# Attention and feed-forward on one core: transposes of q, k and x of batches 4 to 8 moved from TensorE to the DMA, and a reordered start

## The chip, the cores and the metric

The kernel runs on one core of a Trainium2 chip. The metric is the device time of one execution in microseconds (us). The profile's span is a little shorter than that time (348.7 us where the profiled program took about 350), because it counts from the first to the last recorded event. Engines are named as in the profile: PE is TensorE (PEld its weight loads), DVE is VectorE, ACT is ScalarE, POOL is GpSimd, SP is the engine that here only issues DMAs. A "q" behind a name (SPq) is that engine's instruction queue. The text counts batches from 1, the code from 0.

## The reference, cut to what matters

```python
# q, k, v: (8, 8, 576, 64), moe_w_in: (512, 2048), moe_w_out: (2048, 512), float32
scores = scale * np.matmul(q, k.transpose(0, 1, 3, 2))
# heads 0..3 ("plain"):   key is one of the last 32 positions
# heads 4..7 ("dilated"): key is one of the last 128 positions, and (q - k) % 4 == 0
scores = np.where(masks[None, :, :, :], scores, -1e9)
attn = softmax(scores)                       # cut
x = np.matmul(attn, v).transpose(0, 2, 1, 3).reshape(4608, 512)
h = x @ w_in
return (h * sigmoid(h)) @ w_out              # (4608, 512) float32
```

Two things follow. Scores need q and k with the 64 head elements on the partitions, and `x @ w_in` needs x with its 512 features on the partitions; what comes from memory and what attention gives has tokens on the partitions. So q, k and x have to be transposed. And only a narrow band of scores is needed, so attention is small beside the feed-forward part: 1152 matmuls of 512 columns.

## The kernel before: the parts that matter here

All steps of attention (transposes, scores, products with v) and all steps of the feed-forward part (four matmuls each) are put into one order for TensorE by a small plan inside the kernel. The plan simulates engines with given step lengths and given arrival times of the loads. TensorE then runs its instructions strictly in that order, so a step that the plan placed too early holds up everything behind it.

```python
ARRIVE = {0: (8.5, 15.0), 1: (33.0, 47.0)}      # the plan's arrival of q,k and of v, batches 1 and 2
AT_WIN = [19.5, 22.0, 24.5, 27.0]
AT_WOUT = [36.0, 38.5, 41.0, 43.5]
...
def trans_d(ring, h):                            # q and k of a dilated head: 6 transposes on TensorE
    tps = small(ring, [P, 2, 3, MA], F16, f"td_{b}_{h}")
    for rp in range(2):
        for i, key in enumerate(("k", "rest", "q")):
            nc.tensor.transpose(tps[:, rp, i], loads[b][key][:, HN + h, 2 * rp : 2 * rp + 2, :],
                                ident[:MA, :MA])
    yield "DVE", 0.40
    nc.vector.tensor_copy(kqD[:, h]..., tps...)  # PSUM to SBUF
# trans_a, trans_b: 24 transposes a batch for the plain heads, copied on ACT
# x_p, x_d: 28 transposes a batch of the attention output x, copied on DVE (first batch: ACT)
...
def scores(ring, u):                             # matmuls, exp on ACT, then the mask:
    nc.vector.tensor_tensor(pm, pm, mk, ALU.mult)
...
def l1(f):                                       # feed-forward, first layer: a group of 512 tokens
    for c in range(HP):
        nc.tensor.matmul(h, w_in16[:, c, f * P : (f + 1) * P], xT[:, c, t0 : t0 + GT], ...)
    # tanh on ACT, product on DVE into gT
```

So TensorE does 48 transposes of q and k and 28 of x in every batch. All loads are issued by POOL, as DMAs that also cast float32 to float16.

The softmax here doesn't subtract the row's maximum and nothing guards it: scores larger than these inputs give would overflow.

## Time and profile before

| | before |
|---|---|
| time, median of 3 runs | 349.93 us |
| span of the profile | 348.7 us |
| TensorE busy | 325.1 us (93%) |
| first feed-forward matmul | 29.3 us |
| feed-forward matmuls between 100 and 200 us | 349 of 1152 |

The first lines of the profile's page: busy time of each engine, then rows of 40 slices of the span, each digit a tenth of the slice; PEclk is the clock granted to TensorE. The last line is from the chain that ended last.

```profile
PE 325.1 (93%) x2656; PEld 165.1 (47%) x2656; DVE 221.7 (64%) x602; ACT 168.5 (48%) x322; POOL 53.1 (15%) x74
PE   0688898999989999999999999999999999999995
PEclk9999998999999999999999999999999999999999
DMA  8999999929913972990589110100111200201232
PE 84%; DVE 9%; ACT 3%; DMA 2%; issue 1%; POOL 1%; ACTq 0%; POOLq 0%
```

TensorE is the limit: from about 105 us on its row shows nothing but nines until the last slice. The DMA engines are nearly full in the first 70 us and mostly idle from about 190 us on. That idle resource is what the change wants to use.

The timeline of TensorE at the start (start us, length us, line, operation, out<-in, shapes, count, and in brackets the idle time before it with what ended it), and one piece of the chain near the end. `h` and `y` are the two feed-forward layers, `td`, `ta`, `tb` transposes of q and k, `xp`, `xd` of x, `s` the scores, `av` the products with v:

```profile
11.30 0.24 PE L290 MATMUL td_0_205<-ident,rest_111 96*128 96x96 f16 x1 [4.41 <-DMA rest_111<-in_q_dram]
...
29.28 1.90 PE L498 MATMUL h_0_520<-xT,w_in_83 128*128 128x512 f16 x4
30.97 1.91 PE L498 MATMUL h_1_525<-xT,w_in_83 128*128 128x512 f16 x4
...
341.18 3.47 PE y_3_4542 L526 x16
```

TensorE waits until 11.3 us for the last of q and k, and starts its first feed-forward step at 29.3 us. The starts of the first two steps lie 1.69 us apart, against 0.86 us for the same four matmuls later (3.45 us for 16): until then TensorE ran at half speed. The Trainium skill, "TensorE: Matmul & The Clock Gate", section "What's actually happening", says that half clock is the default state and that sustained activity over a window of about 3.4 us releases it. This trace agrees with the two levels, 1.69 and 0.86 us.

### The profile page before, as it was taken

To read this page: it belongs to the slowest core of one execution; us is meant where nothing else is said; L and a number is where in the kernel's file an instruction comes from. 1 tells how busy PE (TensorE), PEld (TensorE's weight loads), DVE (VectorE), ACT (ScalarE), POOL (GpSimd) and SP (SyncE) were. 2 spreads that over 40 slices of the span, in tenths; PEclk is the share of its full clock that TensorE was granted. 3 is DMA by queue.
4 is the path that set the end of the run, shared out by engine and by line. 5 is a ranking of instruction groups with operands and counts; after the bars stand their busy time and mean duration, and the time that the engine had idled before them with its cause. 6 is when DMAs were issued, how large, how long until landed. Compare 5 with 4: busy or idle time off the path is not lost.

```text
span 348.7 us, 6693 instructions
## 1 busy us (share of the span) xinstructions
PE 325.1 (93%) x2656; PEld 165.1 (47%) x2656; DVE 221.7 (64%) x602; ACT 168.5 (48%) x322; POOL 53.1 (15%) x74
## 2 busy tenths in 40 slices
PE   0688898999989999999999999999999999999995
PEld 0553444555445455445554555455545444444442
DVE  4394777758888895888498739883986255054100
ACT  1453664076457546554644464546554254244211
POOL 8724344020203302030311000000000000000000
PEclk9999998999999999999999999999999999999999
DMA  8999999929913972990589110100111200201232
GB/s 107 188 205 199 200 181 169 189 53 141 109 30 37 178 55 59 132 120 32 89 127 103 31 36 27 32 32 30 32 31 32 60 11 22 77 14 32 61 82 70
DMA packets 59920, 29.80 MB, mean 85 GB/s; under 512 B 26608, under 2 KB 55280, under 8 KB 59888
## 3 DMA queue, kind: packets, MB, share of 16 engines
q0 software_dynamic: 54256, 19.92, 51.5%
q1 hardware_dynamic: 5632, 9.44, 9.1%
q8 instruction: 21, 0.34, 0.4%
q14 instruction: 11, 0.09, 0.1%
HBM read 39.84 MB, written 9.44 MB: 141 GB/s over the span
## 4 chain that ended last, share of the span: by engine, by line
PE 84%; DVE 9%; ACT 3%; DMA 2%; issue 1%; POOL 1%; ACTq 0%; POOLq 0%
DMA rest_111<-in_q_dram 2%; DVE gT_1066 L509 1%; PE y_1_892 L526 1%; PE y_3_3599 L526 1%; PE y_3_3089 L526 1%; PE y_3_2568 L526 1%; PE y_2_965 L526 1%; PE y_0_2117 L526 1%; PE y_0_664 L526 1%; PE y_3_4542 L526 1%; PE y_2_2464 L526 1%; PE y_2_2984 L526 1%; PE y_1_3338 L526 1%; PE y_1_3848 L526 1%; PE y_2_3495 L526 1%; PE y_3_1985 L526 1%
## 5 line engine op out<-in xcount | busy, mean ns | idle before, releaser
L498 PEld LDWEIGHTS <-w_in_83 128*128 128x128 f16 x576 | 52.8, 98 | 57.2 <-issue 6.1
L526 PEld LDWEIGHTS <-gT_4055 128*128 128x128 f16 x64 | 6.3, 98 | 7.5
L526 PEld LDWEIGHTS <-gT_3654 128*128 128x128 f16 x64 | 6.3, 98 | 7.6
L526 PEld LDWEIGHTS <-gT_4267 128*128 128x128 f16 x64 | 6.2, 97 | 7.6
L526 PEld LDWEIGHTS <-gT_3144 128*128 128x128 f16 x64 | 5.9, 98 | 6.4
L526 PEld LDWEIGHTS <-gT_519 128*128 128x128 f16 x64 | 5.8, 101 | 6.3 <-issue 1.4
L105 POOL DMA_DIRECT2D vraw_100<-in_v_dram x8 | 5.4, 678 | 20.7 <-DVE vd_98 L359 18.3
L105 POOL DMA_DIRECT2D vraw_101<-in_v_dram x8 | 5.4, 678 | 20.5 <-DVE vd_99 L359 14.7
L526 PEld LDWEIGHTS <-gT_1066 128*128 128x128 f16 x64 | 5.7, 98 | 5.8 <-DVE gT_1066 L509 0.4
L526 PEld LDWEIGHTS <-gT_2629 128*128 128x128 f16 x64 | 5.6, 97 | 5.1
L526 PEld LDWEIGHTS <-gT_2070 128*128 128x128 f16 x64 | 5.6, 97 | 5.1
L526 PEld LDWEIGHTS <-gT_1525 128*128 128x128 f16 x64 | 5.5, 97 | 4.9
L290 PE MATMUL td_0_205<-ident,k_nat_115 96*128 96x96 f16 x2 | 0.5, 272 | 6.6 <-DMA k_nat_115<-in_k_dram 6.6
L121 POOL DMA_DIRECT2D vp_97<-in_v_dram x4 | 5.7, 1432 | 1.5 <-DMA q_nat_167<-in_q_dram 1.4
L121 POOL DMA_DIRECT2D vp_96<-in_v_dram x4 | 5.8, 1444 | 0.6 <-PE td_3_678 L290 0.5
L290 PEld LDWEIGHTS <-rest_111 96*128 96x128 f16 x32 | 3.5, 108 | 5.1 <-issue 4.5
L311 PEld LDWEIGHTS <-kP_106 64*128 64x128 f16 x96 | 3.1, 100 | 5.7 <-issue 5.4
L273 ACT COPY kP_106<-ta_0_224 128x384 f16<-128x384 f16 x1 | 0.5, 479 | 10.9 <-PE ta_0_224 L270 10.9
L509 DVE SCALAR_TENSOR_TENSOR gT_4267<-th_0_4281,h_0_4268 128x512 f16<-128x512 f32 x1 | 0.7, 689 | 7.9 <-ACT th_0_4281 L507 7.9
L328 PEld LDWEIGHTS <-kqD_105 64*128 64x128 f16 x128 | 2.9, 97 | 5.8 <-issue 5.1
L365 PEld LDWEIGHTS <-probs_86 128*128 128x128 f16 x48 | 4.1, 100 | 3.1 <-DVE o_d_199 L368 0.8
L328 PEld LDWEIGHTS <-kqD_104 64*128 64x128 f16 x128 | 3.2, 102 | 5.2 <-issue 4.7
(1782 smaller groups left out, 1014.7 us busy)
## 6 DMA issues: line engine op xcount, KB each, us to landing
w_in_83<-in_moe_w_in_dram POOLq DMA_DIRECT2D x4, 512.0 KB, 12.1
w_out_84<-in_moe_w_out_dram POOLq DMA_DIRECT2D x4, 512.0 KB, 16.2
vp_97<-in_v_dram POOLq DMA_DIRECT2D x4, 384.0 KB, 10.8
vp_96<-in_v_dram POOLq DMA_DIRECT2D x3, 384.0 KB, 6.4
vraw_100<-in_v_dram POOLq DMA_DIRECT2D x4, 224.0 KB, 5.5
vraw_101<-in_v_dram POOLq DMA_DIRECT2D x4, 224.0 KB, 8.3
rest_111<-in_k_dram POOLq DMA_DIRECT2D x4, 192.0 KB, 6.2
rest_111<-in_q_dram POOLq DMA_DIRECT2D x4, 192.0 KB, 7.7
```

The costliest lines, as they stand in the source:

```text
L105: nc.gpsimd.dma_start(out=vraw[p0 : p0 + m1 - m0, ab].rearrange("p h r d -> p h (r d)"), in_=src[m0:m1],)
L121: nc.gpsimd.dma_start(out=vp[:, j0:, :D], in_=win)
L273: nc.scalar.copy(kt[:, :MA], tps[:, 0].rearrange("p r m -> p m r"))
L290: nc.tensor.transpose(tps[:, rp, i], loads[b][key][:, HN + h, 2 * rp : 2 * rp + 2, :], ident[:MA, :MA],)
L311: nc.tensor.matmul(sp[i][:, QB * jj : QB * (jj + 1)], kP[r, hp, QB * j : QB * j + P], qP[r, hp, :, QM * j : QM * (j + 1)], start=True, sto ...
L328: nc.tensor.matmul(sp[i][:, c : c + MH], kqD[r, h, rp, 0, ab * KB : ab * KB + P], kqD[r, h, rp, 1, ab * MH : (ab + 1) * MH], start=True, s ...
L365: nc.tensor.matmul(a[:, i, : D + 1], lhs(i), rhs(i), start=True, stop=True)
L498: nc.tensor.matmul(h, w_in16[:, c, f * P : (f + 1) * P], xT[:, c, t0 : t0 + GT], start=(c == 0), stop=(c == HP - 1),)
L509: nc.vector.scalar_tensor_tensor(gTs[g][:, f], th, 1.0, h, ALU.add, ALU.mult)
L526: nc.tensor.matmul(y, gTs[g][:, f, tb * P : (tb + 1) * P], w_out16[:, f], start=(f == 0), stop=(f == NFF - 1),)
```

## The change

Its intent: take the transposes of the last five batches off TensorE and give them to the DMA, which has time; and start the feed-forward part sooner. The parts:

- q and k of batches 4 to 8 are cast by a DMA into scratch memory in DRAM (`kq_s`) and come back through four transposing DMAs a batch. The plain heads are read as overlapping rows of 128 elements, so that two heads can use the two halves of TensorE's rows.
- x of batches 4 to 8 is stored to DRAM scratch (`x_s`) and comes back transposed, one DMA a feed-forward group.
- The first batch comes in two halves (dilated heads first), its mask is added into the scores by a matmul with the identity before `exp` instead of a multiply on DVE after it, and the first 512 tokens of the feed-forward part are two groups of 256.
- Loads are reordered, and the stores of the output go from SP to ACT.
- In all batches: scores are put into other sets, a copy out of PSUM goes to DVE or ACT as the plan has time, x is kept in the order of tokens, and attention may run further ahead of the feed-forward part.

The core of the diff:

```diff
+    GROUPS = [(0, GT // 2), (GT // 2, GT // 2)] + [(t, GT) for t in range(GT, NT, GT)]
+    PEB = 3                     # q, k: batches 0..2 on TensorE
+    PEX = 3                     # x: the same
+    BIASED = (0,)
...
+    def issue_cast(b):
+        for i, src in enumerate((k, q)):
+            nc.gpsimd.dma_start(out=kq_s[b][i]..., in_=src[b]...)
+    def issue_turn(b, n):       # n = 0..3: plain k, plain q, dilated k, dilated q
...
+            nc.sync.dma_start_transpose(out=dst[:, None, :], in_=win)
...
+            nc.sync.dma_start_transpose(out=kqTs[b % 2][:, i], in_=rows)
...
-    issue_qk(0)
+    issue_first(HN, H)
     make_identity(nc, ident)
...
+    issue_first(0, HN)
...
+    AT_DIL = {0: 7.6, 1: 33.5, 2: 53.0}
+    AT_PLAIN = {0: 11.0, 1: 33.5, 2: 53.0}
+    AT_WOUT = [38.0, 40.5, 47.5, 50.0]
...
+    def turn_gen(b):
+        for n, us in enumerate((3.0, 3.0, 1.5, 7.5)):
+            issue_turn(b, n)
+            yield "DMA", us
...
+    def loads_gen(b):
+        last = max(b - 1, PEB)
+        for i in range(2):      # POOL waits here until the batch before is transposed
+            nc.gpsimd.tensor_copy(fence[:, i : i + 1], kqTs[last % 2][:, i, 1, HN * M - 1 :])
+        if b - 2 >= PEX:
+            nc.gpsimd.tensor_copy(fence[:, 2:3], x_of(first_of[b - 2])[:, HP - 1, GT - 1 :])
+        issue_vraw(b)
+        issue_vp(b)
+        if b > PEB:
+            issue_cast(b)
...
+            if biased:
+                for i in range(2):
+                    nc.tensor.matmul(sp[i]..., ident, bs, start=True, stop=False)
...
-                nc.sync.dma_start(out=rows[r, m : m + n], in_=ob[p : p + n])
+            nc.scalar.dma_start(out=out[t0 + tb * P : t0 + (tb + 1) * P], in_=ob)
```

## The prediction

> **What bounds the kernel now.** TensorE. The engine table gives it 325.1 of 348.7 us; the chain of waits puts 84% of the span on it, 9% on VectorE, 2% on DMA. The granted clock is near 1.0 throughout. 1152 matmuls of 512 columns are needed whatever the change does; the 16 of one y tile take 3.45 us in the undisturbed end of the kernel, 0.216 us each, together 248.5 us. The other 100 us are, by start-to-start differences in the timeline:
> - attention on TensorE, 7 to 7.3 us a batch where nothing waits (stretch 208 to 243): 1.85 for the products with v, 1.89 for the scores, and 3.35 for transposes (q, k: 0.69 + 0.44 + 1.11; x: 0.58 + 0.53). Eight batches: 58 us;
> - the start: the first feed-forward matmul begins at 29.3 us, with only about 7 us of warm-rate work done, so 22 us are lost. The q, k loads end at 11.2 us and delay everything;
> - slow first feed-forward matmuls (four-matmul steps of 1.71 us instead of 0.86), waits up to 100 us and small waits later: about 15 us;
> - the end, last matmul to last byte: 4 us.
>
> **What the change does.**
> 1. Batches 4 to 8 lose all 76 transposes a batch on TensorE, and their PSUM copies on VectorE and ScalarE: 5 x 3.35 = 16.7 us of TensorE time, on the critical path because TensorE never idles after 100 us.
> 2. The DMA takes them over: per batch 1.77 MB of q, k (the plain heads written twice) and 0.59 MB of x through transposing DMAs, plus a cast through DRAM. The Trainium skill, "DMA: Bandwidth & Descriptors", section "Latency and other measured facts", gives 261 GB/s for a transposing DMA in one kernel; estimate 9 us a batch, perhaps 15 with latencies, against a cadence of 35.6 us per group. The slices show DMA 10% to 20% busy from 200 us on and about 60% busy in 100 to 180, so it should fit. The trace of before has no transposing DMA, so this step is the least certain.
> 3. First batch: half of q, k comes first, so transposes start near 7 us instead of 11.3; the first group has 256 tokens and needs half a batch. I expect the first feed-forward matmul at 20 us, bounded by v and the first quarter of w_in. 9 us earlier, but 4 us of attention move behind it and the bias matmuls cost 1 to 2 us. Net 3 to 4 us, and 3 to 5 us fewer waits up to 100 us, since loads are ordered by need.
> 4. VectorE and ScalarE lose work (masks of batch 1, pairing, transposed copies): not critical, worth 1 us. New waits on transposing DMAs, and ScalarE issuing the output stores: minus 1 to 3 us.
>
> **Sum.** 350 - 16.7 - 3.5 - 4 - 1 + 2 = about 326; with some further gain from the longer lead of attention, 324 us. Range 314 to 335. Faster by over 2%: 0.93; within 2%: 0.05; slower: 0.02.
>
> **What would show it.** TensorE instructions down by 380 in transposes (2656 to about 2330, the narrower first groups and bias matmuls adding some); steady groups of 512 tokens at about 32 us instead of 35.6; first h at 18 to 22 us; span about 323; VectorE busy near 195 us; a transposing queue of about 12 MB.
>
> **What would make it wrong.** Transposing DMAs several times slower than estimated, or queued behind stores on the same issuing queue, so that h tiles wait on DMA each batch and the chain shows DMA from 130 us on; w_out late because loads were reordered; the clock staying low longer in the narrow first groups.

## More of the kernel before

Busy time by stretch (columns: stretch and length, busy us and instructions of PE, PEld, DVE, ACT, POOL, then granted clock, DMA share, GB/s; the DMA share sums whole packets' times and so can exceed 1). The last two lines count single source lines in 100 to 200 us, L498 (feed-forward, first layer) and L526 (second layer), PE and PEld only:

```profile
0.00:20.00 20.00, 8.00 (x105) 6.19 (x106) 9.71 (x43) 7.44 (x18) 14.35 (x26) 1.00 1.26 155
20.00:40.00 20.00, 16.43 (x130) 9.02 (x128) 13.94 (x41) 8.65 (x21) 7.51 (x9) 1.00 1.33 202
40.00:60.00 20.00, 18.31 (x178) 9.39 (x178) 15.58 (x41) 12.13 (x25) 8.99 (x11) 0.95 1.91 179
100.00:200.00 100.00, 99.97 (x933) 51.59 (x932) 79.31 (x220) 55.73 (x107) 16.65 (x21) 1.00 0.65 87
...
100.00:200.00 100.00, 49.01 (x192) 16.79 (x192) 1.00 0.65 87
100.00:200.00 100.00, 39.51 (x157) 13.76 (x158) 1.00 0.65 87
```

## The result, and the profile after

The changed kernel took 322.7 us (median of 4 runs, 321.4 to 323.02) against 350.07 us (4 runs, 348.23 to 350.62) for the kernel before. The ratio of the two is 0.9233, with a 95% interval from 0.9198 to 0.9267. Ratios here are the mean time of one kernel's fast runs over that of the other's fast runs of the same rounds, so they are not quite the ratio of the medians.

```profile
PE 304.2 (95%) x2402; PEld 156.4 (49%) x2402; DVE 198.6 (62%) x496; ACT 164.8 (51%) x299; POOL 54.0 (17%) x87
PE   1989599999999999999999999999999999999994
PEclk9998799999999999999999999999999999999999
DMA  7999999996999739998999799952270000100221
PE 83%; DMA 7%; POOL 3%; DVE 2%; ACT 2%; issue 1%; ACTq 0%; POOLq 0%
q1 hardware_dynamic: 52952, 14.75, 25.5%
```

The DMA row is now nearly full until about 210 us. The last line is the queue of SP: 14.75 MB, of which the 20 stores of x of 144 KB are 2.95 MB and the transposing DMAs the other 11.8 MB. TensorE remains the limit. The same stretches as before, and the same count of the two layers (now L851 and L884):

```profile
0.00:20.00 20.00, 13.24 (x204) 9.22 (x204) 12.91 (x43) 12.08 (x23) 17.77 (x33) 1.00 1.18 132
20.00:40.00 20.00, 15.04 (x151) 12.59 (x151) 13.44 (x41) 10.31 (x27) 8.35 (x11) 0.84 1.41 197
40.00:60.00 20.00, 19.40 (x247) 12.67 (x245) 17.41 (x57) 13.99 (x36) 5.40 (x7) 0.99 1.86 189
100.00:200.00 100.00, 100.00 (x780) 47.97 (x779) 71.82 (x178) 52.08 (x83) 14.56 (x24) 1.00 1.08 175
...
100.00:200.00 100.00, 50.60 (x205) 18.35 (x204) 1.00 1.08 175
100.00:200.00 100.00, 47.76 (x196) 17.79 (x195) 1.00 1.08 175
```

TensorE was just as busy between 100 and 200 us as before, with 780 instructions instead of 933. What counts is which: 401 of them were feed-forward matmuls (205 + 196), before 349 (192 + 157). One group of 512 tokens (128 matmuls) therefore takes 128 x 100 / 401 = 31.9 us instead of 36.7. This is the sentence to keep in mind when reading a busy row: both are full, and one does 15% more of the feed-forward work. The count isn't the gain itself, for it also depends on how much attention falls into the stretch: the kernel below with all transposes back on TensorE has 338 in it, fewer than the kernel before, and is 9.5 us faster.

At the start:

```profile
6.75 0.24 PE L522 MATMUL td<-ident,xR 96*128 96x96 f16 x1 [6.75 <-DMA xR<-in_q_dram]
...
21.09 0.61 PE L851 MATMUL h<-xA,w_in 128*128 128x256 f16 x4 [0.63 <-ACT probs L612]
...
26.16 6.94 PE L851 MATMUL h<-xA,w_in 128*128 128x256 f16 x60
...
36.70 0.93 PE L505 MATMUL td<-ident,nat 96*128 96x96 f16 x11 [3.56 <-DMA nat<-in_q_dram]
37.43 1.05 PE L851 MATMUL h<-xA,w_in 128*128 128x256 f16 x4
```

TensorE starts at 6.75 us and reaches the feed-forward part at 21.1 us, 8.2 us sooner than before. The clock record shows full clock from 16.4 us on, with two half-clock periods of 3.4 us, at 23.2 and at 36.9 us. The second follows a hole of 3.56 us, in which TensorE, after one transpose of k of batch 2, stood before the first that needs q, while narrow `h` steps of the second group, which didn't need batch 2, stood ready behind it: the plan expected q and k of batch 2 at 33.5 us, and q came at 36.7.

And what waits for the transposing DMAs? First one batch on SP's queue (start us and length of the issue; the transpose of x among them belongs to an earlier batch), then who waits on the results, from the list of waits of POOL, and TensorE's first scores of that batch (6). A `fence` is a copy of one column by POOL that waits for transposed data, so that POOL's next loads come after it:

```profile
136.73 2.17 SPq L153 DMA_TRANSPOSE nat<-kq_s  x1
139.01 1.92 SPq L407 DMA_TRANSPOSE xR<-x_s  x1
140.99 2.69 SPq L153 DMA_TRANSPOSE nat<-kq_s  x1
143.78 2.83 SPq L156 DMA_TRANSPOSE kqT<-kq_s  x2
...
POOL fence L384 <- DMA kqT<-kq_s: 95.4, 8, 23.2
...
150.63 0.35 PE L599 MATMUL s<-nat 64*128 64x96 f16 x8
```

TensorE's own list of waits has no transposing DMA in it. Only POOL waits, 95 us in eight waits for q and k (and 11 us in two for x), before it issues the next batch's loads and cast. So the transposes are hidden from TensorE, but not by much: for batch 6 the last of the four had landed at 148.8 us (the fence copy on POOL), and the first scores that need the batch began at 150.6 us. In batches 5 and 7 the room was 2.1 and 1.2 us.

### The profile page after: what moved, and what is told of

It reads as the page before. It is cut to its first block, busy times and chain, and to the rows that moved or that the text cites. A ratio compares the mean times of both kernels' runs of the same rounds, so it can differ in the third digit from the quotient of the medians.

```text
span 321.2 us, 6143 instructions
## 1 busy us (share of the span) xinstructions
PE 304.2 (95%) x2402; PEld 156.4 (49%) x2402; DVE 198.6 (62%) x496; ACT 164.8 (51%) x299; POOL 54.0 (17%) x87
## 3 DMA queue, kind: packets, MB, share of 16 engines
q1 hardware_dynamic: 52952, 14.75, 25.5%
## 4 chain that ended last, share of the span: by engine, by line
PE 83%; DMA 7%; POOL 3%; DVE 2%; ACT 2%; issue 1%; ACTq 0%; POOLq 0%
PE y L884 38%; PE h L851 36%; DMA nat<-in_q_dram 5%; PE s L599 3%; DMA vp<-in_v_dram 2%; PE av_d L646 2%; PE av_p L646 2%; DVE oD L650 1%; POOL nat L128 1%; PE td L505 1%; ACT ob L895 1%; ACT probs L608 0%; DVE probs L617 0%; PE ta L480 0%; POOL nat L117 0%
## 5 line engine op out<-in xcount | busy, mean ns | idle before, releaser
L884 PE MATMUL y<-w_out,gT 128*128 128x512 f16 x576 | 138.1, 379 | 0.0
L862 DVE SCALAR_TENSOR_TENSOR gT<-th,h 128x512 f16<-128x512 f32 (+1 forms) x160 | 98.9, 629 | 58.6 <-ACT th L860 58.3
L860 ACT ACTIVATE th<-h 128x512 f32<-128x512 f32 (+1 forms) x160 | 88.6, 556 | 80.6 <-PE h L851 73.3
L851 PEld LDWEIGHTS <-w_in 128*128 128x128 f16 x640 | 59.2, 99 | 54.0 <-issue 1.7
L884 PEld LDWEIGHTS <-gT 128*128 128x128 f16 x576 | 54.0, 98 | 60.0
L851 PE MATMUL h<-xR,w_in 128*128 128x512 f16 x320 | 77.2, 379 | 0.2 <-DVE gT L862 0.2
L851 PE MATMUL h<-xA,w_in 128*128 128x512 f16 (+1 forms) x320 | 66.9, 345 | 0.6 <-ACT probs L612 0.6
L608 ACT ACTIVATE probs<-s 128x768 f16<-128x768 f32 (+2 forms) x46 | 36.0, 782 | 21.6 <-PE s L599 19.9
L650 DVE TENSOR_TENSOR oD<-av_d,rcps 72x256 f16<-72x256 f32 x64 | 26.9, 421 | 2.2
L646 PEld LDWEIGHTS <-probs 128*128 128x128 f16 x448 | 21.7, 99 | 13.2 <-DVE probs L617 1.4
## 6 DMA issues: line engine op xcount, KB each, us to landing
kq_s<-in_k_dram POOLq DMA_DIRECT2D x5, 576.0 KB, 10.7
kq_s<-in_q_dram POOLq DMA_DIRECT2D x5, 576.0 KB, 13.2
```

Of the source, the lines that this page charges most:

```text
L608: nc.scalar.activation(p2, both[:, :, :n], AF.Exp, scale=scale)
L646: nc.tensor.matmul(a[:, i, : D + 1], lhs(i), rhs(i), start=True, stop=True)
L650: nc.vector.tensor_tensor(o, a[:n, :, :D], rcp[:n, :, None].broadcast_to([n, HN, D]), ALU.mult)
L851: nc.tensor.matmul(h[:, :w], w_in16[:, c, f * P : (f + 1) * P], x_g[:, c], start=(c == 0), stop=(c == HP - 1),)
L860: nc.scalar.activation(th[:, :w], h[:, :w], AF.Tanh, scale=0.5)
L862: nc.vector.scalar_tensor_tensor(gTs[g][:, f, :w], th[:, :w], 1.0, h[:, :w], ALU.add, ALU.mult)
```

## The experiments

Twelve kernels ran. The theories:

- A: the removed transposes were on the critical path one for one, and the DMA path that replaces them is hidden. Rival B: most of the gain is in the first 60 us, and the DMA path pays part of its gain back.
- For the start, C: TensorE's order is out of step with the loads, and that costs time. D: the loads are the limit there, whatever TensorE does.

Where I give a difference to the changed kernel below, it is the difference of the two ratios to the kernel before, times 350 us. The intervals of a ratio are about plus or minus 0.3 to 0.7%, that is 1.1 to 2.5 us; a difference of two ratios is less sure than either, by about 1.6 to 2.8 us. The kernel before had medians of 349.29 to 350.07 us in the three sets of runs and the first one.

### x back on TensorE

```diff
-    PEX = 3
+    PEX = 8
```

(and x in one array for all groups; to make room, the transposed dilated q and k share the memory of their older form).

> The changed kernel, with x of batches 4 to 8 transposed on TensorE again (28 transposes a batch, q and k still by DMA). Theory A, that the removed transposes were on the critical path one for one and the DMA path is hidden: 5 x (0.53 + 0.58) = 5.5 us slower than the changed kernel, about 328 us. Rival B, that most of the gain is in the first 60 us and the DMA path pays back part of what it saves through waits: within 2 us of the changed kernel, 321 to 325 us.

Measured: 329.37 us, ratio 0.9416, correct; 6.4 us slower than the changed kernel. Theory A said 5.5.

### q and k back on TensorE

```diff
-    PEB = 3
+    PEB = 8
+    def nat_gen(b):             # load q, k when the scores of batch b - 2 are done
+        issue_nat(b, 0, H)
+        yield "DMA", 13.0
+        nat_in[b].done = plan.now
```

> The changed kernel, with q and k of batches 4 to 8 loaded and transposed on TensorE again (48 transposes a batch), x still by DMA. Theory A: 5 x (0.69 + 0.44 + 1.11) = 11.2 us slower than the changed kernel, about 334 us. Rival B: under 5 us slower.

Measured: 342.85 us, ratio 0.9827, and a wrong result (relative error 0.11). Its number answers nothing: TensorE had stood before a feed-forward step, as its timeline shows:

```profile
230.00 1.89 PE L851 MATMUL h<-xR,w_in 128*128 128x512 f16 x4 [5.25 <-DMA xR<-x_s]
```

I took it for my own fault (argued; the run below, correct and without that wait, fits it): with q and k ready sooner, attention runs further ahead, and one of three buffers of transposed x is written for a later group while an earlier one still has steps to come. The mended kernel has five buffers:

```diff
-    XR = 3
+    XR = 5
```

> The run with q and k back on TensorE, mended. The first try gave a wrong result and stood 5.25 us at 230 us on a transposing DMA into one of the three x buffers[...]: with q and k ready sooner, attention ran further ahead, and a buffer of x was written for a later group while an earlier group still needed it. Five x buffers instead of three take both away. Theory A: 11.2 us slower than the changed kernel, about 334 us, correct, and no such wait. Rival B (most of the gain is in the start): under 5 us slower.

Measured: 336.5 us, ratio 0.9638, correct, and no such wait; 14.2 us slower than the changed kernel (interval of the ratio 0.9571 to 0.9705; with the changed kernel's own, about 11.5 to 16.8). Theory A said 11.2, a little under the interval.

### No transposing DMA at all

Both edits together. What is left of the change is its start and the parts that hold in all batches (the last point under "The change").

> The changed kernel without any transposing DMA: 76 transposes a batch back on TensorE in all batches; what is left of the change is the order of loads, the first batch in two halves, the narrow first groups and the bias. Theory A: 16.7 us slower than the changed kernel, about 339 us, so some 10 to 11 us faster than the kernel before. Rival B: 325 to 331 us.

Measured: 339.63 us, ratio 0.9728, correct; 17.3 us slower than the changed kernel, where theory A said 16.7. Its page and one stretch:

```profile
PE 319.1 (94%) x2782; PEld 170.2 (50%) x2782; DVE 215.0 (64%) x551; ACT 188.9 (56%) x379; POOL 57.4 (17%) x82
100.00:200.00 100.00, 99.95 (x1021) 53.27 (x1018) 81.60 (x219) 64.34 (x133) 13.22 (x16) 1.00 0.53 73
```

It has 380 TensorE instructions more than the changed kernel, exactly 5 x 76, and 1021 instead of 780 in the steady stretch. Theory A holds and rival B falls: of 26.8 us (1 - 0.9233, times 350), 17.3 are the transposes and 9.5 all the rest. The traces put most of the rest early: counting two feed-forward matmuls of 256 columns as one, this kernel starts its 256th at 108.7 us, the kernel before at 116.5, which is 7.8 us of lead; 10.4 us are left at the last one (333.6 and 344.0). The two halves measured alone, 6.4 and 14.2 us, add up to 20.6; within the intervals that is the same as 17.3.

### Filling the hole at 33 us

```diff
-    AT_DIL = {0: 7.6, 1: 33.5, 2: 53.0}
+    AT_DIL = {0: 7.6, 1: 37.0, 2: 53.0}
-    AT_PLAIN = {0: 11.0, 1: 33.5, 2: 53.0}
+    AT_PLAIN = {0: 11.0, 1: 37.0, 2: 53.0}
```

> The changed kernel with one number of its plan altered: batch 2's q and k are expected at 37.0 us instead of 33.5. In the profile TensorE stands 3.6 us at 33 us, before batch 2's first transpose, while feed-forward steps of the second group are ready behind it, and runs at half rate for about 3 us after. Theory C, in-order TensorE blocked by a plan that is too early: 3 to 5 us faster, about 318 us, and no wait over 1 us there. Rival D, the loads are the limit and the wait only moves to w_out at 43 to 50 us: within 1 us of the changed kernel.

Measured: 322.18 us, ratio 0.9236: no change that the runs can resolve. Waits of TensorE and two stretches:

```profile
PE y L884 <- DMA w_out<-in_moe_w_out_dram: 2.9, 2, 1.5
...
20.00:40.00 20.00, 16.79 (x188) 14.06 (x188) 18.19 (x53) 13.97 (x37) 8.51 (x10) 1.00 1.36 199
40.00:60.00 20.00, 16.95 (x208) 10.05 (x207) 12.92 (x43) 10.41 (x27) 5.12 (x7) 1.00 1.63 194
```

The hole is gone (0.30 us are left of it) and the clock is full in the whole stretch. But the work that filled it was work that the changed kernel used between 40 and 60 us: there this one is idle for 3 us, the changed kernel for 0.6. Its new waits are those for w_out, 2.9 us in two waits that end at 39.9 and 42.4 us. The hole, in a stretch that waits for loads, was only moved. Rival D was right here, though in the trace w_out was waited for earlier than it said (43 to 50 us).

### The same with w_out planned later

```diff
-    AT_WOUT = [38.0, 40.5, 47.5, 50.0]
+    AT_WOUT = [40.0, 42.6, 47.5, 50.0]     # and 36.0 instead of 37.0 above
```

> As fill_hole (batch 2 planned at 36.0 us), and the first two quarters of w_out planned at 40.0 and 42.6 us, where fill_hole waited for them, so that attention of batch 2 is put ahead of them. Theory C (a plan out of step with the loads): the two waits of 1.35 and 1.53 us go, 2 to 4 us faster than the changed kernel, 319 to 321 us. Theory D (in the first 60 us the loads are the limit, whatever the order on TensorE): within 1.5 us of it.

Measured: 321.12 us, ratio 0.9201 (0.9146 to 0.9256); 1.1 us faster than the changed kernel, less than the interval. The two waits for w_out did go (0.5 us are left of 2.9, and 0.7 of the hole), and still C's 2 to 4 us didn't come: again D fits better than C. It has the lowest median of all correct kernels, but the runs don't show that it is faster than the changed kernel.

### Fewer bytes in the first 50 us

One quarter of w_out is loaded and used four times. Its output is wrong, which doesn't matter for the time. The plan isn't quite the one of the filled hole: q and k of batch 2 are planned at 36.0 us, as in the last run, and all of w_out at 40.0.

```diff
     for f0 in range(0, NFF, 4):
         ...
+        if f0 > 0:
+            continue
         nc.gpsimd.dma_start(out=w_out16[:, f0 : f0 + 4], in_=wo[:, f0 : f0 + 4])
...
-                    w_out16[:, f],
+                    w_out16[:, f % 4],
```

> Wrong result on purpose: fill_hole's plan, but only the first quarter of w_out is loaded and used in place of all four, so 3.1 of 4.2 MB of reads are taken out of the first 50 us; the same matmuls run. Theory D (loads limit the first 60 us): 3 to 6 us faster than fill_hole, 316 to 319 us. Rival C: no more than 1.5 us faster than fill_hole.

Measured: 318.43 us, ratio 0.9112; 4.3 us faster than the run with the filled hole (0.9236), inside D's 3 to 6. Against the last run (0.9201), whose plan is nearer and which ran in the same rounds, it is 3.1 us, with an interval of about 0.5 to 5.7. Taking away 3.1 MB of reads gives a little more than any order tried on TensorE.

### The first batch loaded in one piece

```diff
-    issue_first(HN, H)
+    issue_first(0, H)
...
-    issue_first(0, HN)
...
-    AT_DIL = {0: 7.6, 1: 33.5, 2: 53.0}
+    AT_DIL = {0: 11.0, 1: 33.5, 2: 53.0}
```

> The changed kernel with q and k of the first batch loaded in one piece again, all heads at once, and so planned (11.0 us). The first transpose on TensorE should come at about 11 us instead of 6.75. Theory D (the loads limit the first 60 us; TensorE has slack there): under 2 us slower. Rival H (an earlier start counts one for one): 3 to 4.5 us slower.

Measured: 325.63 us, ratio 0.931; 2.7 us slower (5 rounds). TensorE's first two marks:

```profile
10.54 0.24 PE L521 MATMUL td<-ident,xR 96*128 96x96 f16 x1 [10.54 <-DMA xR<-in_q_dram]
...
24.26 0.61 PE L850 MATMUL h<-xA,w_in 128*128 128x256 f16 x4
```

It starts 3.8 us later and reaches the feed-forward part 3.2 us later, and 2.7 of them stay. This lies between the two expectations. It is over D's limit of 2, but with an interval of about 1.1 to 4.3 not clearly so. It suggests that theory D isn't the whole truth: the loads limit the stretch from 35 to 60 us, but what happens before that counts too.

### No bias matmul

```diff
-    BIASED = (0,)
+    BIASED = ()
-    nc.vector.tensor_scalar(band, band, 1.0, BIG, ALU.subtract, ALU.mult)
-    nc.vector.memset(mask_p[:W, :2], -BIG)
+    nc.vector.memset(mask_p[:W, :2], 0.0)
```

> The changed kernel without the bias matmuls: batch 1 is masked by a multiply on VectorE as in the other batches. The 14 bias matmuls took 3.9 us of TensorE before the first feed-forward matmul, 0.6 to 0.8 us a pair at half clock; the multiplies take about 0.5 us each on VectorE, seven of them. My prediction said the bias costs 1 to 2 us. If it does: 1 to 2 us faster. If TensorE has slack there (theory D) or VectorE becomes the longer path: within 1 us or slower.

Measured: 326.15 us, ratio 0.934; 3.7 us slower (interval about 1.8 to 5.6). My prediction had the bias as a cost of 1 to 2 us. It is a gain. From the timeline of this run (the slowest of its six, 328.66 us):

```profile
20.39 0.62 PE L645 MATMUL av_p<-vp,probs 128*128 128x65 f16 x8 [0.46 <-DVE probs L616]
23.00 2.42 PE L850 MATMUL h<-xA,w_in 128*128 128x256 f16 x12 [0.44 <-DVE rcps L648]
```

Two things differ from the changed kernel. Attention of the first batch now waits for DVE in several places, and the first feed-forward step comes at 23.0 us instead of 21.1, although TensorE has 3.9 us less to do before it (0.8 us of the delay is the first load, which here landed at 7.55 us instead of 6.75). And the clock record grants full clock only from 25.0 us on, instead of 16.4: the 12 narrow matmuls above take about 0.2 us each, against 0.11 in the changed kernel. It looks as if the dense bias matmuls also bring the full clock sooner: in the traces of all twelve kernels that have them it comes between 10.7 and 17.8 us, in the two that haven't at 25.0 and 33.9, a few us after their first feed-forward matmul. The Trainium skill, "TensorE: Matmul & The Clock Gate", section "Part 4: PE-mode transpose", says that transposes don't count as activity for the clock in the same way; that the kernel before, with its transposes and small matmuls, reached full clock only at 33.9 us agrees with it. But in three traces of kernels with the bias (`double`, `less_wout`, `double_told`) the full clock came in the midst of the first batch's transposes, at 10.7, 12.1 and 12.5 us, after only 1.2 us of bias matmuls, so the runs don't settle it; and no run here separates the shorter chain from the sooner clock.

### Every transposing DMA of q and k twice

```diff
         for n, us in enumerate((3.0, 3.0, 1.5, 7.5)):
             issue_turn(b, n)
+            issue_turn(b, n)
             yield "DMA", us
```

> The changed kernel with every transposing DMA of q and k issued twice in a row (same data, so the result is right), its plan unchanged. From the trace a batch's four take 13 to 16 us from first issue to last landing, and the last lands only 0.9 to 3 us before its first use in batches 5 to 8. Theory E, that the DMA path is hidden by a plan cut close: the second copies wait for the first, some 10 to 13 us per batch are not hidden and TensorE, in order, waits for them: 30 to 60 us slower than the changed kernel, waits on kqT or nat in each batch. Rival F, that there is room to spare because TensorE has other work: under 5 us slower.

Measured: 394.74 us, ratio 1.1295, correct; 72 us slower, more than the 30 to 60 expected. TensorE's waits:

```profile
PE s L600 <- DMA nat<-kq_s: 20.8, 4, 7.1
PE h L852 <- DMA xR<-x_s: 11.3, 2, 9.3
...
PE s L600 <- DMA kqT<-kq_s: 4.8, 2, 3.0
```

With smaller ones, the waits from 78 us on add up to 51 us, and half clock comes with them, 61 us in the record from 79 us on. At half clock, 61 us do the work of about 30. The "room to spare" of rival F doesn't exist. But is it the plan, that doesn't know of the second copies, or the DMA path itself?

```diff
-            yield "DMA", us
+            yield "DMA", 2 * us
```

> As double (every transposing DMA of q and k twice), but the plan that fixes TensorE's order is told twice the time for each. The run double was 72 us slower than the changed kernel: waits of TensorE for transposed data, 51 us in the trace from 78 us on, and 61 us at half clock after them. Theory E (transposing DMAs cost only where the plan doesn't know of them): within 10 us of the changed kernel, 322 to 332 us, few waits on nat or kqT. Rival G (the transposing DMAs of one batch don't fit into one batch's time even if known): over 20 us slower than it.

Measured: 404.56 us, ratio 1.1595, correct: slower still, by 10 us. Theory E falls and rival G stands. Waits of TensorE and POOL's fences on the transposed data (start us):

```profile
PE h L852 <- DMA xR<-x_s: 41.1, 4, 16.1
...
93.34 0.19 POOL L385 COPY fence<-kqT 128x1 f16<-128x1 f16 x1 [5.54 <-DMA kqT<-kq_s]
146.23 0.19 POOL L385 COPY fence<-kqT 128x1 f16<-128x1 f16 x1 [5.89 <-DMA kqT<-kq_s]
192.78 0.19 POOL L385 COPY fence<-kqT 128x1 f16<-128x1 f16 x1 [4.11 <-DMA kqT<-kq_s]
242.87 0.19 POOL L385 COPY fence<-kqT 128x1 f16<-128x1 f16 x1 [6.60 <-DMA kqT<-kq_s]
```

A batch now comes out of the DMA path every 46 to 53 us. In the changed kernel the same fences are here:

```profile
148.76 0.19 POOL L384 COPY fence<-kqT 128x1 f16<-128x1 f16 x1 [0.82 <-DMA kqT<-kq_s]
152.17 0.79 POOL L139 DMA_DIRECT2D kq_s<-in_k_dram  x1
162.88 8.16 SPq L153 DMA_TRANSPOSE nat<-kq_s  x2
178.48 0.19 POOL L384 COPY fence<-kqT 128x1 f16<-128x1 f16 x1 [2.35 <-DMA kqT<-kq_s]
```

These four lines are a loop, and it is what the share of busy DMA engines doesn't show. The transposes of batch 6 land (148.8), then POOL issues the loads of v and the cast of batch 7 (152.2), the cast lands and the transposes start (162.9), they land (178.5), and so on: 29.7 us this turn, one step after another by the fences and the dependence of cast and transpose. It is the shortest turn: the two before it, by the same fences at 77.6, 110.6 and 148.8 us, took 33.1 and 38.1 us, the longer one with 8.9 us in which POOL waited for transposed x. SP's queue holds the stores of x as well, and at 136.7 and 162.9 us the transposes went out right behind one that had waited for attention, so not all of a turn is the DMA's. TensorE needs 144 x 100 / 401 = 35.9 us for the feed-forward matmuls of a batch and everything between them. The mean turn is 33.6 us, so the loop has little to spare, some 2 us in the mean and 6 in its shortest turn, and doubling the transposes adds more: in the told run one batch's transposes took from 65.3 us to the fence at 93.3, 28.1 us, against 12.4 us (65.15 to 77.56) in the changed kernel. Whether bandwidth or the wait of each second copy for the first makes them so long isn't settled; SP's list of waits in this run has 46 us of waits for the copy before. That the told run is slower than the untold one I can only argue: its plan starts attention later, so x is stored later, and TensorE waits for x (41 us and 8.7 us in one more wait) instead of for q and k.

### x of batch 3 by DMA too

```diff
-    PEX = 3
+    PEX = 2                     # and fill2's plan
```

> Meant to beat both kernels: fill2's plan, and x of batch 3 also by transposing DMA (28 transposes fewer on TensorE). Theory A: 0.53 + 0.58 = 1.1 us faster than fill2, about 320 us, 2.7 us faster than the changed kernel. If x of batch 3 comes too late for its group, TensorE waits near 80 to 90 us and it is slower than fill2.

Measured: 321.56 us, ratio 0.9207 (0.9165 to 0.9248), correct. Neither the expected 1.1 us over fill2 nor a wait on x near 80 to 90 us is there; the difference expected is below what the runs resolve, and the try to beat the changed kernel stays undecided. Its six runs lie between 319 and 324 us, wider apart than the gain sought.

## Why the prediction was right, point by point

- The time: 324 us predicted, 322.7 measured. The sum of the terms was "about 326"; the 2 us of "further gain from the longer lead of attention" no run tried alone.
- "5 x 3.35 = 16.7 us of TensorE time, on the critical path": right. Without the transposing DMAs the kernel is 17.3 us slower. That number also holds the transposed copies that DVE and ACT lose, which the prediction counted elsewhere (in 1 us with other work).
- "The DMA takes them over ... estimate 9 us a batch, perhaps 15 with latencies": 12 to 16 us for the four of one batch, near the "perhaps 15". The 9 us counted x too; for the four of q and k the same figure makes an estimate of 6.8 us, so they took about twice as long. The Trainium skill, "DMA: Bandwidth & Descriptors", section "Latency and other measured facts", from which the 9 us came, gives 261 GB/s. Here 1.77 MB in 12 to 16 us is 110 to 148 GB/s, latencies and other traffic included.
- "... against a cadence of 35.6 us per group. The slices show DMA 10% to 20% busy ..., so it should fit": it did fit, but the reason was not good enough. I compared a transfer time with a cadence and looked at the busy share. The limit is the loop of load, cast and transpose, whose turns took 30 to 38 us. That it fit was in part luck: the last transposes landed 1.2 to 2.1 us before their first use in batches 5 to 7. The run with doubled transposes, 72 us slower, shows how near that edge is.
- "the first feed-forward matmul at 20 us": 21.1.
- "the bias matmuls cost 1 to 2 us": wrong in sign. They gain 3.7 us. I costed an added TensorE instruction by its length and forgot that DVE, which it relieves, stood in the chain of the first batch, and that the matmuls may help to bring the clock up. Which of the two makes the gain isn't shown.
- "Net 3 to 4 us, and 3 to 5 us fewer waits up to 100 us": together 6 to 9 us, measured 9.5 for everything but the transposes; taken away alone, the halves cost 2.7 and the bias 3.7 us. This agreement is partly luck: without the 3.7 us of the bias the rest gives 5.8 us, where the prediction, with its 1 to 2 us for the bias taken out, had 7 to 11. What the narrow groups, the order of the other loads and the moved output stores give was not tried alone.
- "New waits on transposing DMAs ...: minus 1 to 3 us": none on TensorE. With the bias these are errors of some us to the slow side; others went the other way, and only 1.3 us are left between prediction and result.
- The marks: groups of 512 tokens at 31.9 us ("about 32", with the warning above about this count), VectorE 198.6 us busy ("near 195"), transposing DMAs 11.8 MB ("about 12"). TensorE instructions came to 2402 instead of "about 2330": 380 fewer, but 64 more from narrow groups, 14 from the bias and 48 from transposing the first batch in smaller pieces.

## What to carry to other kernels

Where TensorE is full in a steady stretch, an instruction taken off it is worth its start-to-start time (here 16.7 us by that count, 17.3 measured), and it can be given to an idle engine even by way of DRAM; but check the replacement as a loop of dependent steps against the time of one turn, not as a busy share. Before filling a hole on TensorE, see whether the stretch behind it waits for loads (here 3.56 us filled gained nothing that the runs resolve). And an added instruction may pay if it takes a step out of another engine's chain: cost it there too.

## What the Trainium skill lacked or had wrong

- "DMA: Bandwidth & Descriptors", section "Latency and other measured facts": 261 GB/s for transposing DMAs was too high for these single transfers, latencies and other traffic included. Here 590 KB of plain q or k landed 5.9 us after issue (median), 295 KB of dilated q or k after 4.5 us, and the four of a batch came to 110 to 148 GB/s beside other traffic.
- None of its pages that I read gives a time for a casting DMA from DRAM to DRAM. Here 576 KB written (twice that read) took 10.7 us for k and 13.2 us for q, issued just after each other (medians).
- "TensorE: Matmul & The Clock Gate", section "Part 4: PE-mode transpose", says that the full clock doesn't engage for transposes. As far as their own speed goes, the transposes here do get it: in the kernel before, those of 96 columns start 0.08 us apart at 15 us and 0.04 us apart at 44 us, when the clock is full. Whether they bring the full clock up the runs leave open (33.9 us in the kernel before, 25.0 us without the bias matmuls, 10.7 to 17.8 us in the twelve traces with them).
